# Dilated-window attention into a token/channel mixer: batch 2's q and k turned by DMA transposes, and batch 2's steps placed anew

## The chip, the cores and the metric

One core of one Trainium2 chip. The metric is the device time of one execution in microseconds (us), the median of the runs. Inputs and output are float32 in DRAM; inside, the kernel works in float16 with float32 sums in PSUM.

## What is computed

Batch 8, 8 heads, 576 positions, head size 64 (512 channels). The reference, cut to what matters:

```python
scores = matmul(q, k.T) / 8                       # per batch and head
rel = i - j                                       # heads 0-3: 0 <= rel < 32
                                                  # heads 4-7: 0 <= rel < 128 and rel % 4 == 0
attn = softmax(where(mask, scores, -1e9))
x = attn @ v                                      # [8, 576, 512], heads side by side
h = relu(x.T @ w_tok1) @ w_tok2                   # mixes positions, 576 -> 256 -> 576
u = x + h.T
out = u + relu(u @ w_ch1) @ w_ch2                 # mixes channels, 512 -> 1536 -> 512
```

## The kernel before, in words

The work goes batch by batch, and all engines but TensorE work ahead of or behind it. For one batch b:

- **Loads.** SP issues the loads of q, k (tiles `l_q`, `l_k`, two halves of four heads each, and `lt` for the last 64 positions) and of v (`l_vn`, four DMAs; `l_vt`, the last 64 positions; `l_vd`; `l_vx`), lines 187 to 245. The weights w_ch1 (`w3`, in thirds) and w_ch2 (`w4`, in thirds, `load_w4`, line 983) are issued by POOL, which casts to float16 on the way.
- **Casts.** `cast_steps` (line 275) gives 17 casts to float16, all on POOL: the tails of q and k, then q and k of the four head pairs in turn, then the eight of v.
- **Turns.** q and k are wanted with the head's channels on partitions. Batches 0 and 1 use `transposes` (line 304) on TensorE. Batch 2 uses `turn_steps` (line 406): `unpad` (line 381) makes four TensorE transposes for each of q and k of the four head pairs and copies them from PSUM by ACT or DVE; `turn_tails` (line 396) does the tails. Batches 3 to 7 use `dma_steps` (line 348): five DMA transposes on SP's queue (tails, then q and k of head pairs 0 and 1, then of 2 and 3), and `place_steps` (line 367): six copies by POOL that put the keys into order.
- **Scores.** For b of 2 and more, `scores_twin` (line 509) runs twice: g = 0 for head pairs 0 and 1 (plain window), g = 1 for pairs 2 and 3 (dilated). It takes six PSUM banks: two of `sc`, three of `fl`, one of `main`. ACT makes eight exps of it, then POOL multiplies by the masks (`mask`, line 566).
- **Values** (line 589): 8 heads, matmuls by TensorE, a reciprocal and a product by DVE. **Token mix**: `emit_h1` (line 618) and `emit_u` (line 629), where "summed" says that x is added by an identity matmul on TensorE and ACT copies, instead of an addition on DVE. For b of 2 and more u is turned by a DMA transpose (`uT_dma`), and `uT_place` has ACT copy half of it into order (line 697).
- **Channel mix.** `gen_first` (line 746): 12 blocks mb of `gp` matmuls (line 767), each into one `main` bank, with a relu on ACT or DVE (line 770); in odd batches three groups `gt` (line 758) for the tails of two batches. `gen_second` (line 776): `yp` chains of 12 matmuls over all of w4, an addition by DVE and the store by SP. The three `main` banks go round in turn.

**What sets the order.** Each engine takes its instructions in the order in which the program emits them. The channel mix is a generator that yields after each piece what the piece costs TensorE; `interleave` (line 819) adds these up as t and emits a step when t has reached the step's place:

```python
steps = sorted(steps, key=lambda st: st[0])
...
    if steps and (main is None or steps[0][0] <= t):
        _, cost, fn = steps.pop(0)
        fn()
        t += cost
```

So a step's place sets its position in the lists of all engines that it uses, the DMA queues of SP and POOL among them. The pass around the change is `firsts()` (line 1007): the first half of batch 1's channel mix, then the second halves of batches 0 and 1, with batch 2's casts, turns, scores, values and token mix, and batch 3's casts, turns and scores placed between (lines 1012 to 1024). The pass ahead of it (lines 1000 to 1005) runs `gen_first(0)` with batch 1's turns, scores, values and token mix between. From line 1030 on one loop does batches 2 to 7.

Of the kernel before, what the change touches and what calls it, by code (L numbers as in the profile page):

```python
# [69 lines left out]
def kernel(  # L70
# [11 lines left out]
    nc = tc.nc  # L82
    sb = ctx.enter_context(tc.tile_pool(name="sb", bufs=1))
    ps = ctx.enter_context(tc.tile_pool(name="ps", bufs=1, space=bass.MemoryType.PSUM))
    SRC = {"q": q, "k": k, "v": v}

    def fixed(name, shape, dtype=FP16):
# [168 lines left out]
    def cast_tails_qk(b, eng):  # L256
        c16[(b, "t")] = sb.tile([128, H, D], FP16, tag="c_t", bufs=1, name=f"c_t_{b}")
        copy(eng, c16[(b, "t")], l32[(b, "t")])

    def cast_tail_v(b, eng):  # L260
        copy(eng, vv[b % 2][0:64, 4, :, 0:64], l32[(b, "vt")])
# [10 lines left out]
    def cast_vx(b, eng):  # L272
        copy(eng, vt[b % 2][:, :, 0:64], l32[(b, "vx")])

    def cast_steps(b, eng=nc.gpsimd):
        steps = [lambda: cast_tails_qk(b, eng)]
        for hp in range(4):
            for nm in ("q", "k"):
                steps.append(lambda nm=nm, hp=hp: cast_qk(b, nm, hp, eng))
        for s in range(4):  # L280
            steps.append(lambda s=s: cast_vn(b, s, nc.gpsimd))
        steps.append(lambda: cast_tail_v(b, nc.gpsimd))
        for h in (0, 2):
            steps.append(lambda h=h: cast_vd(b, h, nc.gpsimd))
        steps.append(lambda: cast_vx(b, nc.gpsimd))
        return steps


# [220 lines left out]
    def scores_twin(b, g):  # L509
# [56 lines left out]
        def mask(hp):  # L566
            if g == 0:
                w = plain_blocks(hp)[:, :, :, 0:BLK]
                mult(nc.gpsimd, w, w, band)
            else:  # L570
                w = attd[hp - 2].rearrange("p h (r c) -> p h r c", c=128)
                mult(nc.gpsimd, w, w, band[:, :, :, 0:128])

        main(2 * g)
        if g:
# [5 lines left out]
        if not g:  # L581
            mask(0)
        t = tail_cols(slice(2 * g, 2 * g + 2), g)
        mult(nc.gpsimd, t, t, tails_seen[g])
        if not g:
            mask(1)
        yield 0.0
# [30 lines left out]
    def emit_h1(b, jb, half, t):  # L618
        x = xn[b]
        j = slice(jb, DTOK, 2)  # L620
        c = slice(256 * half, 256 * half + 256)
        w = w1p if half else w1n
        p = bank("fl", 3, f"h1p_{b}_{jb}_{half}")[:, 0:256]
        nc.tensor.matmul(out=p, lhsT=w1t[b % 2][:, j], rhs=x[:, 4, c], start=True, stop=False)  # L624
        for s in range(4):
            nc.tensor.matmul(out=p, lhsT=w[:, s, j], rhs=x[:, s, c], start=False, stop=(s == 3))  # L626
        relu(nc.vector if jb and (b == 1 or (b == 0 and half)) else nc.scalar, t[:, c], p)

    def emit_u(b, s, h1):
        p = bank("fl", 3, f"up_{b}_{s}")  # L630
        if s < 4:
            summed = b == 1 and s in (0, 2)
            for half in range(2):
                c = slice(256 * half, 256 * half + 256)
                if summed:
# [110 lines left out]
    def gen_first(b):  # L746
# [17 lines left out]
        for mb in range(NMB):  # L764
            p = bank("main", 3, f"gp_{b}_{mb}")
            for i, cb in enumerate(order):
                nc.tensor.matmul(out=p, lhsT=w3_block(cb, mb), rhs=uT[(b, cb)][0], start=(i == 0), stop=(i == 3))  # L767
                if i == 1:
                    yield 0.43
            relu(nc.vector if (mb % 2 == 1 if b == 0 else mb in (1, 5)) else nc.scalar, gta[:, mb, m0:m0 + 512], p)  # L770
            yield 0.43
            if odd and mb in (3, 6, 9):
                gp_tails(mb // 3 - 1)
                yield 0.9
# [168 lines left out]
    def u_half(s, half):  # L943
        p = bank("main" if half else "fl", 3, f"up_0_{s}_{half}")[:, 0:256]
        c = slice(256 * half, 256 * half + 256)
        t = u16(0, s)[:, 2 * half:2 * half + 2]
        summed = s in (0, 2)
        if summed:
            nc.tensor.matmul(out=p, lhsT=ident, rhs=xn[0][:, s, c], start=True, stop=False)
        for jb in range(2):  # L950
# [39 lines left out]
    for i in (0, 1, 2, 3, 4, 5, 7, 6, 8, 9, 10, 11, 12, 13, 14, 15, 16):  # L990
        casts1[i]()
        if i == 1:
            load_w3(2)
        if i in (14, 15, 16):
            load_w4(next(w4s))

    def at(t0, dt, fs):
        return [(t0 + dt * i, 0.0, f) for i, f in enumerate(fs)]

    steps = score_steps(1, 0, 0, (0.0, 0.6, 0.7), (  # L1000
        (2.9, 5.0), (4.2, 6.9), (5.4, 9.3), (8.0, 12.2)))
    va = value_steps(1, 11.3, 0.5)
    steps += va[:4] + [(p + 0.4, c, f) for p, c, f in va[4:]]
    steps += mix_steps(1, 16.0, 17.0, 18.0, 22.6, 0.6)
    interleave(gen_first(0), steps)

    def firsts():
# [1 line left out]
        yield from gen_second(0)  # L1009
        yield from gen_second(1)  # L1010

    steps = at(0, 0.0, [lambda: emit_loads_qk(2)]) + at(1.0, 0.0, [lambda: load_v(2)])
    casts = cast_steps(2)
    steps += at(0, 0.9, casts[:9]) + at(5.8, 0.1, casts[9:])
    steps += turn_steps(2, (5.0, 4.8, 4.2, 6.0, 8.0, 10.3, 9.2, 12.5, 7.9, 7.0),
                        (nc.scalar, nc.vector, nc.scalar, nc.vector, nc.scalar, nc.vector, nc.vector, nc.vector))
    steps += score_steps(2, 10.5, 4.6)
    va = value_steps(2, 19.5, 1.2)
    steps += va[:4] + [(p + 0, c, f) for p, c, f in va[4:]]
    steps += mix_steps(2, 25.5, 29.0, 29.0, 37.0)  # L1020
    steps += at(13.0, 0.0, [lambda: emit_loads_qk(3)]) + at(18.0, 0.0, [lambda: load_v(3)])
    steps += at(18.2, 0, cast_steps(3)) + at(23.0, 0.6, dma_steps(3)) + at(27.0, 0.5, place_steps(3))
    steps += score_steps(3, 35.5, 7.0) + at(33.4, 1.5, load_steps(4))
    interleave(firsts(), steps)

    def both(b):
# [44 lines left out]
```

## Time and profile before

| | |
|---|---|
| median of 3 runs | 286.7 us (286.6 to 286.73) |
| profiled execution | 286.81 us, span 285.0 us |
| PE busy | 273.8 us, 2760 matmuls |
| DVE busy | 132.3 us |
| ACT busy | 131.4 us |
| POOL busy | 166.8 us |
| DMA read, written in HBM | 37.05 MB, 9.44 MB |

The span runs from the first to the last instruction that the profiler shows; the 1.81 us between it and the execution's own time lie around it. PE is TensorE, DVE VectorE, POOL GpSimd, SP SyncE, which issues most DMAs. Times in the rows are us from the span's start unless marked ns. A matmul's duration in a row overlaps the next one's, so the distance between starts tells what it costs. In DMA rows the last number is the time from issue to landing.

### The profile page before, as it was taken

How to read it: one execution, taken by the hardware profiler on the slowest of the kernel's cores; microseconds unless marked ns; L12 is line 12 of the kernel's file. 1: busy time of each engine (PE TensorE's matmuls, PEld its weight loads, DVE VectorE, ACT ScalarE, POOL GpSimd, SP SyncE). 2: the span in 40 equal slices, each digit the busy share in tenths (PEclk: the TensorE clock that was granted, in tenths of full speed). 3: DMA queues.
4: the chain of work that ended last, by engine and by line, in shares of the span. 5: the costliest groups of instructions: out<-in, count | busy, mean ns of one | idle time of the engine just before them, and what ended most of it. 6: DMA issues, size and time to landing. Idle time of an engine off the chain costs nothing.

```text
span 285.0 us, 6873 instructions
## 1 busy us (share of the span) xinstructions
PE 273.8 (96%) x2760; PEld 207.0 (73%) x2760; DVE 132.3 (46%) x280; ACT 131.4 (46%) x263; POOL 166.8 (59%) x236
## 2 busy tenths in 40 slices
PE   5799899999999999999999999999999999999994
PEld 2696576676896976598776976797767966886594
DVE  6875687652365155514730263526531184322022
ACT  2964563458412374473446625482456435134500
POOL 7980853383998769769945998289945900000000
PEclk9999999999999999999999999999999999999999
DMA  7999999999658999999798989399994310521032
GB/s 217 262 227 253 269 230 241 273 223 307 165 105 191 147 332 274 190 168 352 201 191 191 319 241 188 60 235 314 207 148 83 110 39 0 111 93 37 2 86 99
DMA packets 105423, 52.60 MB, mean 185 GB/s; under 512 B 73872, under 2 KB 104208, under 8 KB 105392
## 3 DMA queue, kind: packets, MB, share of 16 engines
q1 hardware_dynamic: 101280, 47.07, 71.2%
q0 software_dynamic: 2512, 3.92, 7.6%
q10 hardware_dynamic: 1600, 1.18, 1.4%
q8 instruction: 21, 0.34, 0.5%
q14 instruction: 10, 0.08, 0.1%
HBM read 37.05 MB, written 9.44 MB: 163 GB/s over the span
## 4 chain that ended last, share of the span: by engine, by line
PE 79%; DMA 9%; POOL 4%; ACT 2%; DVE 2%; issue 1%; SPq 1%; ACTq 0%; POOLq 0%
PE gp L767 26%; PE yp L790 26%; PE h1p L626 4%; PE up L638 4%; PE gt L758 4%; PE yp L810 4%; DMA l_k<-in_k_dram 3%; DMA lt<-in_k_dram 3%; PE sc L519 2%; DMA utm<-u 2%; DMA w<-in_moe_w_tok_dram 2%; POOL attd L113 1%; PE av L605 1%; PE h1p L624 1%; PE av L600 1%
## 5 line engine op out<-in xcount | busy, mean ns | idle before, releaser
L790 PE MATMUL yp<-w,gt 128*128 128x256 f16 x756 | 86.5, 273 | 0.0
L790 PEld LDWEIGHTS <-gt 128*128 128x128 f16 x768 | 78.4, 106 | 6.2
L107 ACT ACTIVATE gt<-gp 128x512 f16<-128x512 f32 x76 | 45.4, 601 | 68.6 <-PE gp L767 68.3
L767 PE MATMUL gp<-utm,w 128*128 128x512 f16 x192 | 67.7, 379 | 0.0
L767 PE MATMUL gp<-utd,w 128*128 128x512 f16 x144 | 54.8, 380 | 0.0
L767 PEld LDWEIGHTS <-w 128*128 128x128 f16 x384 | 39.0, 114 | 20.4 <-issue 1.9
L800 DVE TENSOR_TENSOR o<-yp,u 128x512 f32<-128x512 f32 x31 | 21.4, 691 | 66.5 <-PE yp L790 64.6
L113 POOL TENSOR_TENSOR attp<-attp,const 128x1280 f16<-128x1280 f16 x12 | 31.4, 2615 | 22.4 <-ACT attp L545 18.0
L113 DVE TENSOR_TENSOR xn<-av,rec 128x320 f16<-128x320 f32 x64 | 31.5, 492 | 2.2
L113 POOL TENSOR_TENSOR attd<-attd,const 128x1024 f16<-128x1024 f16 x12 | 25.3, 2129 | 2.4 <-ACT attd L545 2.4
L644 DVE TENSOR_TENSOR u<-up,xn 128x512 f16<-128x512 f32 x26 | 17.5, 689 | 14.1 <-PE up L638 14.0
L103 POOL CAST c_k<-l_k 128x512 f16<-128x512 f32 x29 | 18.0, 623 | 8.8 <-PE tpu L675 7.6
L107 ACT ACTIVATE h<-h1p 128x256 f16<-128x256 f32 x29 | 11.1, 383 | 26.0 <-PE h1p L626 25.7
L103 POOL CAST c_q<-l_q 128x512 f16<-128x512 f32 x31 | 19.6, 635 | 2.6 <-DMA l_q<-in_q_dram 2.6
L545 ACT ACTIVATE attp<-sc 128x480 f16<-128x480 f32 (+1 forms) x36 | 16.1, 528 | 7.4 <-PE sc L519 7.4
L109 DVE TENSOR_SCALAR gt<-gp 128x512 f16<-128x512 f32 x20 | 13.7, 686 | 10.1 <-PE gp L767 10.1
L103 POOL CAST vv<-l_vn 128x256 f16<-128x256 f32 (+1 forms) x40 | 15.0, 403 | 4.0 <-DMA l_vn<-in_v_dram 3.5
L373 POOL COPY kt<-kr 128x512 f16<-128x512 f16 x10 | 10.8, 1079 | 10.4 <-DMA kr<-c_k 6.6
L697 ACT COPY utd<-utm 128x512 f16<-128x512 f16 x12 | 12.7, 1123 | 9.0 <-DMA utm<-u 9.0
L615 DVE RECIPROCAL rec<-av 128x5 f32<-128x5 f32 x64 | 12.2, 190 | 7.4 <-PE av L612 7.0
L545 ACT ACTIVATE attd<-sc 128x512 f16<-128x512 f32 x24 | 12.4, 604 | 6.1 <-PE sc L519 6.1
L758 PEld LDWEIGHTS <-w 128*128 128x128 f16 x192 | 11.9, 113 | 2.0 <-issue 0.4
(149 smaller groups left out, 441.2 us busy)
## 6 DMA issues: line engine op xcount, KB each, us to landing
out_dram<-o SPq DMA_DIRECT2D x72, 128.0 KB, 2.7
l_q<-in_q_dram SPq DMA_DIRECT2D x15, 512.0 KB, 6.9
l_k<-in_k_dram SPq DMA_DIRECT2D x14, 512.0 KB, 7.4
l_vn<-in_v_dram SPq DMA_DIRECT2D x32, 128.0 KB, 6.7
l_vd<-in_v_dram SPq DMA_DIRECT2D x16, 256.0 KB, 4.3
w<-in_moe_w_ch_dram POOLq DMA_DIRECT2D x6, 512.0 KB, 8.3
lt<-in_q_dram SPq DMA_DIRECT2D x8, 128.0 KB, 5.0
l_vt<-in_v_dram SPq DMA_DIRECT2D x8, 128.0 KB, 4.6
```

Source lines behind the costliest of these rows:

```text
L103: eng.tensor_copy(out=out, in_=in_)
L107: nc.scalar.activation(out=out, in_=in_, func=AF.Relu)
L109: eng.tensor_scalar_max(out=out, in0=in_, scalar1=0.0)
L113: eng.tensor_tensor(out=out, in0=x, in1=y, op=ALU.mult)
L545: nc.scalar.activation(out=out, in_=in_, func=AF.Exp, scale=0.125)
L615: nc.vector.reciprocal(out=rec[:, :, 0], in_=av[:, :, 64])
L644: nc.vector.tensor_tensor(out=u16(b, s), in0=blocks4(p), in1=blocks4(xn[b][:, s]), op=ALU.add)
L697: nc.scalar.copy(out=natural(uTd[:, cb - 2]), in_=uTm[i][:, cb].rearrange("p r m -> p m r"))
L758: nc.tensor.matmul(out=p[:, 128 * i:128 * i + 128], lhsT=w3_block(cb, 4 * g + i), rhs=uT[(b, cb)][1], start=(cb == order[0]), stop=(cb == ...
L767: nc.tensor.matmul(out=p, lhsT=w3_block(cb, mb), rhs=uT[(b, cb)][0], start=(i == 0), stop=(i == 3))
L790: nc.tensor.matmul(out=p[:, c], lhsT=gta[:, mb, a0:m0 + 512:4] if half else gta[:, mb, a0:a0 + 128], rhs=w4[mb][:, c], start=(mb == 0), st ...
L800: nc.vector.tensor_tensor(out=blocks4(o32), in0=blocks4(p), in1=u16(b, s), op=ALU.add)
```

## The change

q and k of batch 2 are turned by `dma_steps` and `place_steps`, as in later batches. In the order of emission of the new pass, batch 2's loads of q and k come first, then the nine casts of q and k, the second third of w4, the five turns, the six key copies, the last third of w4, then the loads of v and its casts, of which the tail's is on DVE. (Before, all three thirds of w4 were issued within the casts of batch 1's v, and batch 2's v was loaded right behind its q and k.) One of batch 2's plain masks goes from POOL to DVE. Relus of the channel mix are dealt anew between ACT and DVE: for batch 0, DVE has mb 1 instead of the six odd ones; for batch 1, the six odd ones instead of 1 and 5; later 1, 7, 9 instead of 1 and 5. The relus of the token mix are all ACT's. Identity matmuls stand in u of batch 0 for s = 0, 2, 3 (was 0, 2) and of batch 1 for s = 2 (was 0, 2). The places of the steps are new in both passes.

```diff
--- before.py
+++ after.py
@@ -82,6 +82,7 @@
     nc = tc.nc
     sb = ctx.enter_context(tc.tile_pool(name="sb", bufs=1))
     ps = ctx.enter_context(tc.tile_pool(name="ps", bufs=1, space=bass.MemoryType.PSUM))
+    DVE, ACT, POOL = nc.vector, nc.scalar, nc.gpsimd
     SRC = {"q": q, "k": k, "v": v}
 
     def fixed(name, shape, dtype=FP16):
@@ -272,17 +273,17 @@
     def cast_vx(b, eng):
         copy(eng, vt[b % 2][:, :, 0:64], l32[(b, "vx")])
 
-    def cast_steps(b, eng=nc.gpsimd):
-        steps = [lambda: cast_tails_qk(b, eng)]
+    def cast_steps(b, engs=(nc.gpsimd,) * 17):
+        steps = [lambda: cast_tails_qk(b, engs[0])]
         for hp in range(4):
             for nm in ("q", "k"):
-                steps.append(lambda nm=nm, hp=hp: cast_qk(b, nm, hp, eng))
+                steps.append(lambda nm=nm, hp=hp: cast_qk(b, nm, hp, engs[2 * hp + 1 + (nm == "k")]))
         for s in range(4):
-            steps.append(lambda s=s: cast_vn(b, s, nc.gpsimd))
-        steps.append(lambda: cast_tail_v(b, nc.gpsimd))
-        for h in (0, 2):
-            steps.append(lambda h=h: cast_vd(b, h, nc.gpsimd))
-        steps.append(lambda: cast_vx(b, nc.gpsimd))
+            steps.append(lambda s=s: cast_vn(b, s, engs[9 + s]))
+        steps.append(lambda: cast_tail_v(b, engs[13]))
+        for i in range(2):
+            steps.append(lambda i=i: cast_vd(b, 2 * i, engs[14 + i]))
+        steps.append(lambda: cast_vx(b, engs[16]))
         return steps
 
 
@@ -566,10 +567,10 @@
         def mask(hp):
             if g == 0:
                 w = plain_blocks(hp)[:, :, :, 0:BLK]
-                mult(nc.gpsimd, w, w, band)
+                mult((POOL, DVE)[hp] if b == 2 else POOL, w, w, band)
             else:
                 w = attd[hp - 2].rearrange("p h (r c) -> p h r c", c=128)
-                mult(nc.gpsimd, w, w, band[:, :, :, 0:128])
+                mult((POOL, POOL)[hp - 2] if b == 2 else POOL, w, w, band[:, :, :, 0:128])
 
         main(2 * g)
         if g:
@@ -581,7 +582,7 @@
         if not g:
             mask(0)
         t = tail_cols(slice(2 * g, 2 * g + 2), g)
-        mult(nc.gpsimd, t, t, tails_seen[g])
+        mult((POOL, POOL)[g] if b == 2 else POOL, t, t, tails_seen[g])
         if not g:
             mask(1)
         yield 0.0
@@ -624,12 +625,12 @@
         nc.tensor.matmul(out=p, lhsT=w1t[b % 2][:, j], rhs=x[:, 4, c], start=True, stop=False)
         for s in range(4):
             nc.tensor.matmul(out=p, lhsT=w[:, s, j], rhs=x[:, s, c], start=False, stop=(s == 3))
-        relu(nc.vector if jb and (b == 1 or (b == 0 and half)) else nc.scalar, t[:, c], p)
+        relu(nc.vector if jb and (b < 0) else nc.scalar, t[:, c], p)
 
     def emit_u(b, s, h1):
         p = bank("fl", 3, f"up_{b}_{s}")
         if s < 4:
-            summed = b == 1 and s in (0, 2)
+            summed = b == 1 and s in (2,)
             for half in range(2):
                 c = slice(256 * half, 256 * half + 256)
                 if summed:
@@ -767,7 +768,7 @@
                 nc.tensor.matmul(out=p, lhsT=w3_block(cb, mb), rhs=uT[(b, cb)][0], start=(i == 0), stop=(i == 3))
                 if i == 1:
                     yield 0.43
-            relu(nc.vector if (mb % 2 == 1 if b == 0 else mb in (1, 5)) else nc.scalar, gta[:, mb, m0:m0 + 512], p)
+            relu(nc.vector if mb in ((1,), (1, 3, 5, 7, 9, 11), (1, 7, 9))[min(b, 2)] else nc.scalar, gta[:, mb, m0:m0 + 512], p)
             yield 0.43
             if odd and mb in (3, 6, 9):
                 gp_tails(mb // 3 - 1)
@@ -944,7 +945,7 @@
         p = bank("main" if half else "fl", 3, f"up_0_{s}_{half}")[:, 0:256]
         c = slice(256 * half, 256 * half + 256)
         t = u16(0, s)[:, 2 * half:2 * half + 2]
-        summed = s in (0, 2)
+        summed = s in (0, 2, 3)
         if summed:
             nc.tensor.matmul(out=p, lhsT=ident, rhs=xn[0][:, s, c], start=True, stop=False)
         for jb in range(2):
@@ -991,17 +992,17 @@
         casts1[i]()
         if i == 1:
             load_w3(2)
-        if i in (14, 15, 16):
+        if i in (14,):
             load_w4(next(w4s))
 
     def at(t0, dt, fs):
         return [(t0 + dt * i, 0.0, f) for i, f in enumerate(fs)]
 
-    steps = score_steps(1, 0, 0, (0.0, 0.6, 0.7), (
-        (2.9, 5.0), (4.2, 6.9), (5.4, 9.3), (8.0, 12.2)))
+    steps = score_steps(1, 0, 0, (0.0, 0.6, 1.5), (
+        (2.9, 5.8), (5.0, 7.7), (6.6, 9.3), (8.0, 11.4)))
     va = value_steps(1, 11.3, 0.5)
     steps += va[:4] + [(p + 0.4, c, f) for p, c, f in va[4:]]
-    steps += mix_steps(1, 16.0, 17.0, 18.0, 22.6, 0.6)
+    steps += mix_steps(1, 16.0, 17.0, 18.0, 30.6, 0.0)
     interleave(gen_first(0), steps)
 
     def firsts():
@@ -1009,18 +1010,18 @@
         yield from gen_second(0)
         yield from gen_second(1)
 
-    steps = at(0, 0.0, [lambda: emit_loads_qk(2)]) + at(1.0, 0.0, [lambda: load_v(2)])
-    casts = cast_steps(2)
-    steps += at(0, 0.9, casts[:9]) + at(5.8, 0.1, casts[9:])
-    steps += turn_steps(2, (5.0, 4.8, 4.2, 6.0, 8.0, 10.3, 9.2, 12.5, 7.9, 7.0),
-                        (nc.scalar, nc.vector, nc.scalar, nc.vector, nc.scalar, nc.vector, nc.vector, nc.vector))
-    steps += score_steps(2, 10.5, 4.6)
-    va = value_steps(2, 19.5, 1.2)
-    steps += va[:4] + [(p + 0, c, f) for p, c, f in va[4:]]
-    steps += mix_steps(2, 25.5, 29.0, 29.0, 37.0)
-    steps += at(13.0, 0.0, [lambda: emit_loads_qk(3)]) + at(18.0, 0.0, [lambda: load_v(3)])
-    steps += at(18.2, 0, cast_steps(3)) + at(23.0, 0.6, dma_steps(3)) + at(27.0, 0.5, place_steps(3))
-    steps += score_steps(3, 35.5, 7.0) + at(33.4, 1.5, load_steps(4))
+    steps = at(0.0, 0.0, [lambda: emit_loads_qk(2)]) + at(6.0, 7.5, [lambda: load_v(2)])
+    casts = cast_steps(2, (POOL, POOL, POOL, POOL, POOL, POOL, POOL, POOL, POOL, POOL, POOL, POOL, POOL, DVE, POOL, POOL, POOL))
+    steps += at(0.0, 0.0, casts[:9]) + at(6.5, 0.0, casts[9:])
+    steps += at(0.0, 5.5, [lambda: load_w4(next(w4s))]) + at(5.4, 0.0, [lambda: load_w4(next(w4s))])
+    steps += at(2.0, 0.5, dma_steps(2)) + at(5.1, 0.0, place_steps(2))
+    steps += score_steps(2, 10.0, 3.1)
+    va = value_steps(2, 18.7, 1.2)
+    steps += va[:4] + [(p + 0.0, c, f) for p, c, f in va[4:]]
+    steps += mix_steps(2, 26.6, 29.1, 30.1, 43.0)
+    steps += at(9.5, 6.5, [lambda: emit_loads_qk(3)]) + at(15.5, 0.0, [lambda: load_v(3)])
+    steps += at(17.2, 0, cast_steps(3)) + at(21.0, 0.0, dma_steps(3)) + at(27.0, 0.5, place_steps(3))
+    steps += score_steps(3, 35.0, 4.5) + at(38.4, 0.5, load_steps(4))
     interleave(firsts(), steps)
 
     def both(b):
```

## Rows read from the trace of the kernel before

**Rows 1.** The page's first part: busy time, share of the span, instructions.
```profile
PE 273.8 (96%) x2760; PEld 207.0 (73%) x2760; DVE 132.3 (46%) x280; ACT 131.4 (46%) x263; POOL 166.8 (59%) x236
```
**Rows 2.** Stretches: length, busy PE, PEld, DVE, ACT, POOL (instructions), clock, DMA share, GB/s.
```profile
26.00:54.00 28.00, 26.44 (x292) 18.29 (x290) 20.22 (x45) 13.92 (x29) 13.19 (x25) 1.00 1.12 253
54.00:72.00 18.00, 17.40 (x184) 11.48 (x182) 6.92 (x15) 12.42 (x26) 11.25 (x19) 1.00 1.10 268
...
103.00:280.00 177.00, 176.87 (x1686) 133.13 (x1685) 71.65 (x148) 80.03 (x156) 98.76 (x123) 1.00 0.71 164
```
**Rows 3.** Timeline of TensorE, batch 1's first half: start, us, line, shapes, count.
```profile
54.62 3.71 PE L767 MATMUL gp<-uT,w 128*128 128x512 f16 x16
...
59.07 0.39 PE L385 MATMUL tp_q<-const,c_q 128*128 128x128 f16 x4
59.29 0.59 PE L767 MATMUL gp<-uT,w 128*128 128x512 f16 x2
```
**Rows 4.** Timeline of TensorE, batch 2's scores to batch 3's [idle before <-what ended it].
```profile
66.08 0.23 PE L519 MATMUL sc<-qt,kt 64*128 64x128 f16 x2 [0.20 <-DVE kt L103]
...
68.67 1.05 PE L758 MATMUL gt<-uT,w 128*128 128x128 f16 x16 [0.18 <-ACT attt L545]
...
72.08 3.44 PE L790 MATMUL yp<-w,gt 128*128 128x256 f16 x30
...
91.28 0.65 PE L519 MATMUL sc<-qt,kt 64*128 64x160 f16 x14
```
**Rows 5.** Timeline of TensorE, batch 1's turns in the pass before.
```profile
31.61 0.40 PE L310 MATMUL tp_k<-const,c_k 128*128 128x128 f16 x4 [0.20 <-POOL c_k L103]
32.16 0.40 PE L310 MATMUL tp_q<-const,c_q 128*128 128x128 f16 x4 [0.16 <-POOL c_q L103]
...
34.98 0.38 PE L310 MATMUL tp_k<-const,c_k 128*128 128x128 f16 x4 [0.26 <-DVE kt L103]
```
**Rows 6.** Timeline of ACT: batch 2's first exps, and u's copies ahead of batch 3's.
```profile
65.77 2.23 ACT L545 ACTIVATE attp<-sc 128x480 f16<-128x480 f32 x5
...
99.59 2.08 ACT L697 COPY utd<-utm 128x512 f16<-128x512 f16 x2 [4.98 <-DMA utm<-u]
```
**Rows 7.** DMA issues one by one, 39 to 57 us: queue, size, us to landing.
```profile
l_k<-in_k_dram SPq DMA_DIRECT2D x1, 512.0 KB, 13.6
...
w<-in_moe_w_ch_dram POOLq DMA_DIRECT2D x1, 512.0 KB, 8.2
...
w<-in_moe_w_ch_dram POOLq DMA_DIRECT2D x1, 512.0 KB, 11.8
...
l_vt<-in_v_dram SPq DMA_DIRECT2D x1, 128.0 KB, 4.7
```
**Rows 8.** Timeline of POOL: w4's first third, batch 2's first k, batch 3's first key copy.
```profile
41.33 0.54 POOL L984 DMA_DIRECT2D w<-in_moe_w_ch_dram  x1 [0.19 <-issue]
...
53.62 0.61 POOL L103 CAST c_k<-l_k 128x512 f16<-128x512 f32 x1 [7.58 <-PE tpu L675]
...
88.57 1.06 POOL L373 COPY kt<-kr 128x512 f16<-128x512 f16 x1
```
**Rows 9.** SP: turns (issue ns min/median/max) and landing; four vn; batch 4's turns' stretch.
```profile
L351 SPq DMA_TRANSPOSE qt<-c_q x10: 1253/1455/2196, 81.9 to 206.7; - x10
...
DMA to landing us min/median/max: 3.1/3.9/5.7
...
4.52 3.18 SPq L206 DMA_DIRECT2D l_vn<-in_v_dram  x4
...
112.00:119.00 7.00, 7.00 (x46) 4.26 (x45) 3.26 (x6) 3.30 (x7) 5.47 (x12) 1.00 1.12 219
```
**Rows 10.** The page's fifth part: relus on DVE, busy, mean ns, idle before.
```profile
L109 DVE TENSOR_SCALAR gt<-gp 128x512 f16<-128x512 f32 x20 | 13.7, 686 | 10.1 <-PE gp L767 10.1
```
**Rows 11.** Timeline of POOL and TensorE: batch 3's dilated masks and their first value.
```profile
102.73 4.22 POOL L113 TENSOR_TENSOR attd<-attd,const 128x1024 f16<-128x1024 f16 x2 [2.39 <-ACT attd L545]
...
108.12 0.20 PE L609 MATMUL av<-vt,attt 128*128 128x65 f16 x1
```

## Prediction

> **What bounds the kernel now.** I read the page first, then stretches, then each engine's timeline between 26 and 125 us. TensorE is busy for 96% of the span [rows 1], and from 103 to 280 us for 176.87 of 177.00 us [rows 2]: once batch 2's pass has begun, TensorE has no gap to give. So the end moves by two things alone: work taken from TensorE's list, and waits of TensorE that vanish or appear. Before 103 us there are waits: 1.56 us of idle in 26:54 and 0.60 us in 54:72 [rows 2]. Most edits lie here, and the DMA engines are full here (share 1.12 and 1.10 [rows 2]). So I ask what the edits do to TensorE's list and its waits, and whether the DMA queues can deliver in time. The granted clock is 1.00 in every stretch [rows 2], the 2.4 GHz level, and nothing in the change leaves TensorE idle for long; I leave the clock out. One caution: an idle figure of TensorE counts from the modelled end of the matmul before. Four transposes that began at 31.61 should have let the next start at 31.83; it started at 32.16 with 0.16 of idle shown [rows 5]. So 0.33 us was lost: the idle figure plus 0.17. I add that 0.17 to each wait.
>
> **1. The turns leave TensorE: -2.0 us.** Batch 2 is turned by 32 transposes for q and k and 4 for the tails. A group of four starts at 59.07 and the next matmul at 59.29 [rows 3]: 0.22 us a group, nine groups, 2.0 us. The 0.39 us of the row overlaps its neighbours. They stand amid gp matmuls that run without a pause, so the whole is on the path. The Trainium skill, page "TensorE: Matmul & The Clock Gate", section on PE-mode transpose, measures about 275 ns for one transpose in a kernel; 36 would be 9.9 us and the time 277.1. The rows give 0.055 us each, so the trace disagrees, and I take the rows.
>
> **2. Waits that go with the turns: -0.7 us.** Batch 2's first scores wait at 66.08 for a key copy by DVE (0.20 + 0.17), and the gt group at 68.67 for a bank that ACT's exps hold (0.18 + 0.17) [rows 4]. Whether they come back is part 4.
>
> **3. Batch 1's steps: -0.75 us.** TensorE meets q of head pair 1 at 32.16 (0.33 lost) and k of pair 2 at 34.98 (0.26 + 0.17) [rows 5]. The new places put gp matmuls ahead of both. The wait for the very first k (31.61) stays, because POOL's cast sets it. The relus moved from DVE to ACT cost nothing: ACT is busy 13.92 of 28.00 us in 26:54, DVE 20.22 [rows 2], and five relus more make ACT 17. The identity matmuls are two fewer in batch 1 and two more in batch 0: zero. Batch 0's two lie ahead of TensorE's wait for POOL's first cast of batch 1; the two fewer lie where DVE now adds one more u and holds the bank. The relus that stand on DVE for mb 1, 7, 9 in later batches are off the path.
>
> **4. A new wait at batch 2's scores: +1.8 us.** The tail cast of v goes from POOL to DVE, which takes its instructions in order. What such a wait does, ACT shows at 99.59: it sat 4.98 us for a DMA, with the next exps behind it [rows 6]. When does the tail land? SP issues batch 2's loads, then the five turns, then v. Without two of the three w4 loads beside them, q and k come sooner: k's first half took 13.6 us with w4 in flight [rows 7], which is why POOL's cast ran only at 53.62 [rows 8] (the profile names PE there, but the load landed at that moment). The first w4 (issued at 41.33 [rows 8], 8.2 us [rows 7]) still shares until 49.5, so I put that half at 50.0 and the last at 53.7 (2.0 us per 512 KB at the 253 GB/s of [rows 2]). Three casts later, at 55.4, SP may issue the last turn. A turn costs SP 1.25 to 1.46 us; two follow the cast of q at 54.9, so v begins near 57.5. Its four vn take 3.2 us [rows 9], the tail is issued at 60.6, and 4.7 us later [rows 7] it is here: about 65.2. Then come its cast and, behind it on DVE, the relu of gp 7, at 0.69 each by DVE's nearest row of 512 columns [rows 10]: 66.6. That relu frees the bank which batch 2's small scores want, as the third user after it in the turn of three. The pass begins at 54.62 - 0.75 = 53.9 [rows 3], and by the placing rule TensorE is there 10.9 us later, at 64.8. So it waits 1.8 us. I bound the landing by 63.5 (if k's last half were here at 52) and 66.5 (if the tail took 6 us). There is a floor of 0.8: if v is early, gp 11 waits instead for the bank of the small scores. ACT's eight exps, begun at 65.77, held it until the gt group could start at 68.67 [rows 4, 6], some 2.85 us, and only 1.8 us of matmuls will stand between in place of 2.3. The two overlap, so part 4 is 0.8 to 3.1, not their sum.
>
> **5. The turns by DMA: 0.** Scores want the keys at 64.4. The first halves of q and k are issued by 54.3 and land within 3.9 us of their issue [rows 9], near 57; POOL's copies took under 2.8 us in batch 3 (begun at 88.57 [rows 8], scores at 91.28 [rows 4]), so they end near 60. Cover: 4 us. The last w4 is issued behind those copies, at about 60.5, and lands 8.2 to 11.8 us later [rows 7], at 68.7 to 72.3; its first use is at 72.08 - 1.65 + 0.87 = 71.3 [rows 4]: 0 taken, up to 1.0 kept for the range. The turns also take the DMA engines' time: batch 4's five, with hardly anything beside them, filled the engines from 112 to 119 (share 1.12 [rows 9]). So I let batch 3's loads come 6 us later, its v near 82.5. POOL, with one mask less ahead of them, is at these casts earlier than before and waits for v; I put its last v cast at 86; the key copies (under 2.8 us) end near 89, ahead of 91.5.
>
> **6. POOL and what follows: 0.** One mask goes from POOL to DVE; its price there is not in the trace. By the nearest row, 0.69 for 512 columns [rows 10], 1280 would be 1.7 us; below, half of that; above, double. All are covered, because its values come some 7 us later. In the new order batch 3's scores stand behind three more yp pieces (0.65 us each by the placing rule), so they start 0.3 us after the old 91.28 [rows 4] and POOL has 2 us to spare. Its dilated masks no longer wait for ACT's copies. POOL was free at 102.73 - 2.39 = 100.34, worked until 108.1, 5.3 us in all, and would now end at 105.6. TensorE got them at 108.12 [rows 11], after 0.30 us of waiting, and would now ask at 108.12 - 0.30 - 1.65 = 106.17. Zero, with half a microsecond to spare.
>
> **Sum.** -2.0 - 0.7 - 0.75 + 1.8 = -1.65 us. The profiled execution took 286.81 us (span 285.0, 1.81 around it), which gives 285.16; the median of the runs is 0.11 below the profiled one, so **285.0 us**.
>
> **Rivals.**
> - *Slower: v's tail holds DVE.* Same place as part 4, but v lands so late that the wait eats everything. The gains are 3.45; with 0.57 us (0.2%) for a verdict the wait must pass 4.0 us, the landing 67.4. For it: a transfer of batch 2 took 13.6 us before [rows 7]; against it: the tail took 4.7. At a landing of 69 TensorE waits 5.6 us: 288.8. The Trainium skill, "DMA: Bandwidth & Descriptors", section "Queues, rings and completion order", says that a DMA engine takes turns between its queues packet by packet. By that rule the second w4, issued near 55.5 from POOL, would share with v; k's 13.6 us agrees. Chance 0.12.
> - *w4 late.* TensorE waits for the last third in the first yp chain, 0.5 to 1.5 us: 285.5 to 286.5. For it: 11.8 us once [rows 7]; against it: that was the last of three in a row. Chance 0.12.
> - *The gain isn't carried.* POOL has 0.5 us of reserve at batch 3's masks and 2 us at its keys. If batch 3's loads come 3.5 us later still, TensorE stands at batch 3's scores for 1.2 us: 286.2. Chance 0.12.
> - *It doesn't do what it says:* the transposes only filled waits, so taking them out shows as waits. Then only part 3 is left against part 4: 286.7 - 0.75 + 1.8 = 287.7. Against it: the groups follow one another without a gap [rows 3]. Chance 0.04.
> - *The transposes cost their rows' full time:* nine groups of 0.39 are 3.5 us instead of 2.0, 283.5. Against it: [rows 3] show them overlapping. Chance 0.01.
>
> **How the numbers follow.** The forecast has 0.59, the other cases 0.41. A measurement of this kernel can tell about 0.2%, 0.57 us, from no change, so faster is below 286.13. The forecast's own range is 283.5 (part 4 at 0.8, with half a microsecond of waits elsewhere gone) to 286.3 (part 4 at 3.1). With the w4 rival and the third, 283.5 to 286.8 leaves out 2 in 10. Faster: 0.56 of the forecast, 0.09 of w4, 0.05 of the third, 0.01 of the last: 0.71. Same: 0.03, 0.03, 0.06 and 0.01 of the first: 0.13. Slower: the rest, 0.16.
>
> **What would show it.** Right: no transposes in batch 2's rows; a DVE cast of v's tail that waits for its DMA, and one TensorE wait of 1 to 3 us at batch 2's small scores; the first yp near 70.4 (72.08 before [rows 4]); the same lead of 1.6 us to the end. Wrong: a wait at the first yp (w4), at batch 2's first scores (turns late), at batch 3's scores or dilated values (POOL), or a lead that shrinks after 103 us.

## The result, and the profile after

The changed kernel takes 290.65 us in the median of 6 runs (289.64 to 291.49), the kernel before 286.59 in runs beside it; ratio 1.0147, 95% interval 1.0124 to 1.017. It is slower by 4 us, outside the range that was given. The profiled execution is the fastest of the six, 289.64 us, with a span of 287.9 us. Here and below a time is the median of all runs of a kernel, and a ratio leaves out a run that is over 1.5% above its kernel's fastest (one each in experiments 2 and 10).

The page's first part; it answers to [rows 1]:

```profile
PE 273.7 (95%) x2724; PEld 207.0 (72%) x2724; DVE 131.0 (45%) x273; ACT 128.3 (45%) x259; POOL 167.3 (58%) x240
```

36 matmuls fewer: the turns are gone from TensorE. Its busy time is nearly unchanged, since part of the work now ran at a lower clock (below). The stretches (columns as in [rows 2]), with two short ones between:

```profile
26.00:54.00 28.00, 27.02 (x307) 19.40 (x306) 18.25 (x42) 17.96 (x38) 15.93 (x30) 1.00 1.19 257
54.00:72.00 18.00, 14.43 (x115) 8.60 (x113) 5.82 (x9) 7.34 (x17) 7.24 (x16) 0.94 1.11 185
...
70.00:73.00 3.00, 3.00 (x15) 1.07 (x14) 0.83 (x1) 1.34 (x3) 0.90 (x2) 0.50 1.19 243
73.00:74.00 1.00, 1.00 (x26) 0.80 (x21) 0.00 (x0) 0.56 (x2) 0.96 (x2) 0.90 1.10 331
...
103.00:280.00 177.00, 176.12 (x1679) 132.22 (x1677) 74.69 (x154) 76.28 (x148) 99.97 (x124) 1.00 0.69 165
```

The loss lies in 54:72: TensorE idles 3.6 of 18 us (0.60 before), and the clock falls. The last two columns say where to look: the DMA engines are as busy as before (1.11, before 1.10) but move 185 GB/s, not 268. That is 18 us x 83 GB/s = 1.5 MB less, 5.6 us of the old rate. Not all of it is the turns' doing, since the second third of w4 now lies in this stretch too. Experiment 7, with w4 there and no turns, moves 254, and experiment 3, with the turns and w4 early, 201. The turns' own bytes are in the 185, and they bring in nothing from DRAM. A share of 1.11 doesn't mean that no engine stood idle either: in the first half microsecond of the stretch nothing moved, while SP was issuing a turn. SP's timeline shows what stood behind them:

```profile
48.29 2.56 SPq L352 DMA_TRANSPOSE qt<-c_q  x1
...
54.80 1.27 SPq L352 DMA_TRANSPOSE kr<-c_k  x1
56.13 6.23 SPq L207 DMA_DIRECT2D l_vn<-in_v_dram  x4
62.41 0.62 SPq L207 DMA_DIRECT2D l_vt<-in_v_dram  x1
```

The last turn was issued at 54.80, earlier than the prediction had it (v from 57.5 on; it began at 56.13). But the four vn cost SP 6.23 us, so the tail of v went out at 62.41. The 3.18 of [rows 9] are from the start of the kernel (4.52 us). The same trace has two more rows for four vn, of batches 2 and 3, with busy DMA engines (share 1.06 in 44:54, 1.08 in 63:72) and no turn beside them:

```profile
43.07 12.86 SPq L206 DMA_DIRECT2D l_vn<-in_v_dram  x4
...
64.65 5.39 SPq L206 DMA_DIRECT2D l_vn<-in_v_dram  x4
```

So 6.23 is no odd price for this stretch, and not by itself a sign of the turns. DVE, which casts that tail:

```profile
60.30 0.69 DVE L110 TENSOR_SCALAR gt<-gp 128x512 f16<-128x512 f32 x1 [1.03 <-PE gp L768]
67.55 0.55 DVE L104 CAST vv<-l_vt 64x512 f16<-64x512 f32 x1 [6.57 <-DMA l_vt<-in_v_dram]
68.03 1.26 DVE L110 TENSOR_SCALAR gt<-gp 128x512 f16<-128x512 f32 x2
```

It sat 6.57 us for the load, with a relu behind the cast for which the TensorE bank waited. TensorE, with the same stretch of work as [rows 4]:

```profile
64.53 0.64 PE L520 MATMUL sc<-qt,kt 64*128 64x160 f16 x13
68.75 0.21 PE L520 MATMUL sc<-qt,kt 64*128 64x128 f16 x1 [3.57 <-DVE gt L110]
...
70.04 2.77 PE L768 MATMUL gp<-uT,w 128*128 128x512 f16 x6
72.74 0.82 PE L520 MATMUL sc<-qt,kr 64*128 64x128 f16 x16
...
74.07 2.13 PE L791 MATMUL yp<-w,gt 128*128 128x256 f16 x18
...
123.57 0.44 PE L520 MATMUL sc<-qt,kt 64*128 64x160 f16 x8 [0.88 <-POOL kt L374]
```

TensorE is at the small scores about when forecast (65.2, that is 68.75 less the wait; 64.8) and stands 3.57 us. From 70 to 73 us the granted clock is 0.50, the 1.2 GHz level, with 0.89 in the microsecond before and 0.90 in the one behind: six gp matmuls take 2.77 us, where sixteen took 3.71 [rows 3]. The wait had ended at 68.75, about a microsecond before the fall; nothing else had stopped TensorE since 54. At half clock 3 us hold 1.5 us of work, and with 0.1 lost on either side this costs 1.7 us. One more wait, 0.88 us, follows at batch 4's keys. After it the two traces run alike.

**The account**, in distances within each trace, since the first turn of batch 1 (30.09 before, 30.55 after) starts at a moment that the first loads set:

| stretch of TensorE | before | after | difference |
|---|---|---|---|
| first turn of batch 1 to first gp of batch 1 | 24.53 | 23.38 | -1.15 |
| to the first yp | 17.46 | 20.14 | +2.68 |
| to batch 2's first gp | 31.18 | 30.79 | -0.39 |
| to batch 3's first gp | 29.07 | 29.91 | +0.84 |
| to the end | 148.96 | 148.97 | 0.0 |

The sum is +1.98, with 0.46 from the later start +2.44; the execution is 2.83 longer, and the 0.4 between them lie behind TensorE's last matmul. The forecast had -0.9 in the second line (-2.0 - 0.7 + 1.8). The 3.6 us that it misses there are the wait, 3.57 + 0.17 in place of 1.8, and the clock, 1.7.

### The profile page after: what moved, and what is told of

Same layout as the page of the kernel before. It is cut to its first block, busy times and chain, and to the rows that moved or that the text cites. A ratio compares the mean times of both kernels' runs of the same rounds, so it can differ in the third digit from the quotient of the medians.

```text
span 287.9 us, 6801 instructions
## 1 busy us (share of the span) xinstructions
PE 273.7 (95%) x2724; PEld 207.0 (72%) x2724; DVE 131.0 (45%) x273; ACT 128.3 (45%) x259; POOL 167.3 (58%) x240
## 4 chain that ended last, share of the span: by engine, by line
PE 72%; DMA 14%; SPq 4%; POOL 4%; DVE 2%; issue 1%; ACT 1%; POOLq 0%; ACTq 0%
PE yp L791 26%; PE gp L768 21%; DMA l_vd<-in_v_dram 4%; DMA l_k<-in_k_dram 4%; PE yp L811 4%; PE h1p L627 4%; PE gt L759 3%; PE up L639 3%; PE sc L520 3%; SPq L207 3%; DMA const<-consts 2%; DMA l_vt<-in_v_dram 2%; DMA l_q<-in_q_dram 2%; DMA kr<-c_k 1%; SPq L807 1%
## 5 line engine op out<-in xcount | busy, mean ns | idle before, releaser
L108 ACT ACTIVATE gt<-gp 128x512 f16<-128x512 f32 x71 | 42.3, 597 | 75.3 <-PE gp L768 74.8
L114 POOL TENSOR_TENSOR attp<-attp,const 128x1280 f16<-128x1280 f16 x11 | 28.8, 2616 | 21.0 <-ACT attp L546 20.9
L110 DVE TENSOR_SCALAR gt<-gp 128x512 f16<-128x512 f32 x25 | 17.1, 686 | 30.9 <-PE gp L768 30.9
L108 ACT ACTIVATE h<-h1p 128x256 f16<-128x256 f32 x32 | 12.3, 383 | 24.3 <-PE h1p L627 23.6
L645 DVE TENSOR_TENSOR u<-up,xn 128x512 f16<-128x512 f32 x27 | 18.1, 686 | 1.3 <-PE up L639 0.8
L374 POOL COPY kt<-kr 128x512 f16<-128x512 f16 x12 | 12.9, 1075 | 9.5 <-DMA kr<-c_k 8.6
```

Of the source, the lines that this page charges most:

```text
L108: nc.scalar.activation(out=out, in_=in_, func=AF.Relu)
L110: eng.tensor_scalar_max(out=out, in0=in_, scalar1=0.0)
L114: eng.tensor_tensor(out=out, in0=x, in1=y, op=ALU.mult)
L374: nc.gpsimd.tensor_copy(out=natural(kt[hp][:, 0:512]), in_=kra[:, hp].rearrange("p r m -> p m r"))
L645: nc.vector.tensor_tensor(out=u16(b, s), in0=blocks4(p), in1=blocks4(xn[b][:, s]), op=ALU.add)
```

## The experiments

The theory at the start: v's tail lands late, because SP and the DMA engines are taken by the turns, and whoever waits for v hands the delay to TensorE. Rivals: DVE as the place of the cast is at fault; the order of w4 is; the turns only need to stand elsewhere; batch 4's loads are; or the turns are innocent.

**1. The tail's cast back on POOL.**

```diff
-    casts = cast_steps(2, (POOL, ..., DVE, POOL, POOL, POOL))
+    casts = cast_steps(2)
```

> Edit: the cast of batch 2's v tail goes back from DVE to POOL; all else as in the changed kernel (290.65 us, TensorE idle 3.57 us at batch 2's small scores, clock 0.50 at 70 to 73 us). Theory A, DVE's place in line alone: with DVE free the small scores wait at most 0.8 us, the clock stays at 1.00 and 3 us of waiting and 1.6 us of half clock come back: 285.5 to 286.5 us. Theory B, v is late for whoever waits for it: POOL's v casts end near 73 as now, its masks of batch 2 come behind them (73 to 81.6), and TensorE waits at the values instead, 1.2 us at the first and some 1.6 us at the first dilated one: 288 to 289.5 us.

291.15 us, ratio 1.0164 [1.0114, 1.0213]: no gain, and above both theories' ranges. The profile is of the quickest of the four runs (289.17); the others lie from 290.94 on. TensorE's timeline has no wait for DVE, but these, and two of 1.0 us for POOL's copies of batch 4's keys:

```profile
67.23 0.59 PE L768 MATMUL gp<-uT,w 128*128 128x512 f16 x2 [0.74 <-ACT attt L546]
...
70.45 3.87 PE L791 MATMUL yp<-w,gt 128*128 128x256 f16 x34 [0.53 <-DMA w<-in_moe_w_ch_dram]
...
75.52 0.20 PE L601 MATMUL av<-vv,attp 128*128 128x65 f16 x1 [1.20 <-POOL attp L114]
...
81.42 0.20 PE L610 MATMUL av<-vt,attt 128*128 128x65 f16 x1 [0.94 <-POOL attt L114]
```

The first is the floor of 0.8 that the prediction gave. The waits for POOL's masks are the same delay of v, now passed on by POOL, whose masks stand behind its casts of v. So the wait at DVE was the form of the loss, not its cause.

**2. v ahead of the turns.**

```diff
-    steps = ... + at(6.0, 7.5, [lambda: load_v(2)])
+    steps = ... + at(0.0, 7.5, [lambda: load_v(2)])
```

> Edit: batch 2's v is loaded right behind its q and k, ahead of the five turns, the tail cast still on DVE. By both theories v's tail lands near 60 and DVE does not wait. The turns then stand behind v in SP's list: if SP is held by full queues until about 58, the last turns are issued near 62 and POOL's key copies end near 66 to 68, so TensorE waits 2 to 4 us at the first scores (idle named after POOL kt): 288 to 291 us. If the turns had room after all, no wait: 284.5 to 286 us.

294.35 us (four runs from 291.65 to 297.73), 1.0258 [1.0168, 1.0348], slower than the 288 to 291 expected. Now the turns are late: in the trace TensorE waits 2.95 and 0.95 us at batch 2's scores for POOL's key copies, and 2.04 for w4, and the granted clock of 54:72 is 0.88. Either of these two orders makes something late.

**3. All of w4 early, as before.**

```diff
-        if i in (14,):
+        if i in (14, 15, 16):
```

> Edit: all three thirds of w4 are issued within batch 1's casts, as before the change; all else as changed. Theory C, the second third of w4 sharing the engines with turns and v is what made v late: the last turn lands in 4 instead of 8.2 us, the tail lands near 65 to 66, the wait shrinks by 1.5 to 2 us: 288 to 289 us. Theory D, the line at SP is what made v late: q and k land near 57 again, the casts end near 59, the turns are issued until 60.5, the tail lands near 69 and DVE holds TensorE for 1 to 3 us more: 291.5 to 294 us.

290.75 us, 1.0148 [1.0117, 1.0179]: no difference that can be measured, with 4.9 us of wait for DVE in its trace. Neither range (288 to 289, 291.5 to 294) was met. The stretch and SP's timeline:

```profile
54.00:72.00 18.00, 13.12 (x108) 8.51 (x107) 5.21 (x8) 6.79 (x15) 11.60 (x22) 0.87 1.12 201
```

```profile
54.71 1.35 SPq L352 DMA_TRANSPOSE qt<-c_q  x1
...
61.42 2.91 SPq L207 DMA_DIRECT2D l_vn<-in_v_dram  x4
64.37 0.63 SPq L207 DMA_DIRECT2D l_vt<-in_v_dram  x1
```

Both theories were right in part, and the parts cancel. With w4 out of the way the last turn landed in 4.5 us (8.2 in the changed kernel), the four vn cost 2.91 (6.23), and the tail landed in 3.9 (5.1): near the prediction's prices (3.9, 3.2 and 4.7), though the turns were directly ahead. But w4 now lay beside q and k: the first turn of q went out at 54.71, not 48.29, and the tail at 64.37, not 62.41. So w4 beside the last turns and v is part of what makes v late, and to move it to this place doesn't help.

**4. The tail on POOL, batch 2's large masks on DVE.**

```diff
-                mult((POOL, DVE)[hp] if b == 2 else POOL, w, w, band)
+                mult(DVE if b == 2 else POOL, w, w, band)
...
-                mult((POOL, POOL)[hp - 2] if b == 2 else POOL, w, w, band[:, :, :, 0:128])
+                mult(DVE if b == 2 else POOL, w, w, band[:, :, :, 0:128])
...
+    casts = cast_steps(2)
```

> Edit: as e1, and both plain and both dilated masks of batch 2 on DVE, so that no mask but the tails' stands behind v on POOL. Theory B: the waits at scores and at the plain values are both gone; left is the wait for POOL's tail masks at the values: 285 to 287 us, 2 us or more below e1. Theory A: the masks were not the bound, so the same as e1 within 0.5 us.

291.6 us, 1.0188 [1.0132, 1.0245]; the theory missed its 285 to 287. The profile is of the slowest of the four runs (293.58). POOL's waits at the values are gone, and what was behind them shows: TensorE stands 2.20 us for w4 at its first yp (72.50), then 2.8 us for batch 4's keys.

**5. Batch 4's loads at their old places.**

```diff
-    steps += score_steps(3, 35.0, 4.5) + at(38.4, 0.5, load_steps(4))
+    steps += score_steps(3, 35.0, 4.5) + at(33.4, 1.5, load_steps(4))
```

> Edit: batch 4's loads go back to their old places (33.4, one step every 1.5) from (38.4, every 0.5); all else as changed. Theory E, a second loss behind 103 us: in the changed kernel SP issued batch 4's loads 98.74 to 113.9 us, its turns behind them, and TensorE lost 0.88 us of idle at batch 4's scores (POOL's key copy). With the old places that wait is gone and the time falls by about 1 us, to 289.0 to 290.0 us; the wait at batch 2's scores stays 3 to 4 us. Rival: the turns of batch 4 are late because the whole of POOL and SP is late since batch 2, then the wait stays and the time is 290 to 291 us.

290.85 us, 1.015 [1.0126, 1.0173], with the same two waits (3.9 and 0.9 us). What makes batch 4's keys late by 0.9 us is not the place of its loads.

**6. The first pass's edits alone, on the kernel before** (the relus, the identity matmuls, the places of batch 1's steps).

```diff
-        relu(nc.vector if jb and (b == 1 or (b == 0 and half)) else nc.scalar, t[:, c], p)
+        relu(nc.vector if jb and (b < 0) else nc.scalar, t[:, c], p)
...
-            summed = b == 1 and s in (0, 2)
+            summed = b == 1 and s in (2,)
...
-        (2.9, 5.0), (4.2, 6.9), (5.4, 9.3), (8.0, 12.2)))
+        (2.9, 5.8), (5.0, 7.7), (6.6, 9.3), (8.0, 11.4)))
```

> Edit: the kernel before, with the change's edits of the pass ahead of batch 2 alone: batch 1's steps placed anew, relus of batch 0 and of the token mixes to ACT, the identity matmuls re-dealt. The changed kernel began the next pass 0.69 us earlier (53.93 for 54.62). If that lead is carried to the end: 285.6 to 286.1 us. Rival: POOL's list for batches 2 and 3 is fixed and takes the lead away: 286.3 to 286.7 us.

286.01 us in 12 runs, 0.9979 [0.9966, 0.9991], against 286.47: part 3 of the prediction is worth 0.46 us at the end.

**7 and 8. No turn of batch 2 at all**, in the new order and in the old; the scores read tiles that POOL fills with zeros. The places in 7, then in 8:

```diff
-    steps += at(2.0, 0.5, dma_steps(2)) + at(5.1, 0.0, place_steps(2))
+    steps += at(5.1, 0.0, place_steps(2))
...
-    steps += turn_steps(2, ...)
+    steps += at(7.0, 0.0, [lambda: ends(nc.vector)])
```

> Edit: the changed kernel with batch 2's five DMA transposes left out (its scores read a blank tile that POOL sets to zero while it is idle near 22 us), everything else in place. Theory B, the transposes fill the DMA engines and SP's line when these are full, and whatever is behind them comes late: v lands 4 to 6 us earlier, DVE's tail cast and POOL's masks do not wait, no wait but the 0.8 us floor is left at batch 2's scores: 284.0 to 286.0 us. Rival, the order of w4, v and the casts is at fault and not the transposes: v's tail still lands after 66 and the time is 288 us or more.

> Edit: the kernel before with batch 2's turns left out altogether, the 36 transposes of TensorE and the copies out of PSUM (the same blank tiles). This is the most that any way of turning batch 2 off TensorE can give: 2.0 us of transposes and 0.7 us of waits, 283.5 to 284.3 us. Rival: POOL and DMA set the pace behind TensorE, and less than 1 us comes back: 285.6 us or more.

The new order without turns: 285.8 us, 0.999 [0.9963, 1.0016]. With them the ratio was 1.0147, so the five DMA turns, as placed, cost 1.6%, 4.5 us (4.85 by the medians). The runs lie in two groups, five of 284.27 to 285.26 and five of 286.34 to 287.89, so this is a mean; the profile is of the second (287.44). Its stretch and SP's timeline:

```profile
54.00:72.00 18.00, 16.85 (x166) 10.74 (x164) 8.49 (x11) 10.34 (x22) 11.88 (x20) 1.00 1.10 254
```

```profile
44.99 8.16 SPq L207 DMA_DIRECT2D l_vn<-in_v_dram  x4
53.24 1.04 SPq L207 DMA_DIRECT2D l_vt<-in_v_dram  x1
```

The tail was issued at 53.24 and landed 4.8 us later; in the changed kernel at 62.41 and 5.1. So what the turns take from v is almost all time in SP's line: there SP comes to v at 56.13, and here at 44.99, since it needn't wait for the casts of q and k and issue five turns. The four vn cost even more here, 8.16 us.

The old order without turns: 285.94 us, 0.9985 [0.9966, 1.0003]. So in the old order, to take the turns off TensorE for nothing brings some 0.5 us, not clear of noise, where the prediction counted 2.7. (In the new order the quicker five runs of experiment 7 are 1.2 to 2.2 us below the kernel before; what sets them apart, no trace shows.) TensorE's waits after 54 us in the trace of experiment 8:

```profile
PE yp L790 <- ACT attt L545: 0.9, 1, 0.9
PE sc L519 <- POOL kt L373: 0.7, 1, 0.7
PE av L609 <- POOL attt L113: 0.5, 1, 0.5
```

There ACT's exps, POOL's masks and batch 4's keys stand right behind TensorE. With 0.17 for each wait they take 2.6 of the 2.7 us.

**9. v issued by POOL, not behind the turns on SP.**

```diff
-    steps = ... + at(6.0, 7.5, [lambda: load_v(2)])
+    steps = ... + at(5.0, 7.5, [lambda: load_v(2, POOL)])
...
```

> The changed kernel, but batch 2's eight loads of v are issued by POOL ahead of its key copies, not by SP behind the five turns. Theory L (v is late because it stands in SP's line behind the turns): v's tail is issued near 57 instead of 62.4 and lands near 62 to 63, DVE's cast is in time, the 3.6 us wait at batch 2's small scores shrinks to the 0.7 that ACT's exps set, the clock stays at 1.00, and the time is 286 to 287. Theory E (the turns take the DMA engines' own time, whoever issues beside them): v's tail comes earlier, but the last turn, which landed at 63.0, comes later by about as much, TensorE waits for batch 2's keys instead, and the time stays within 289.5 to 292.

299.03 us, 1.0432 [1.0402, 1.0462]. Theory L fell. E was right that the last turn comes later, but the tail came later too, TensorE still waited for DVE (7.16 us), and the time is far beyond E's range. POOL issued the tail at 57.1. From issue to landing, from the view of the tile of v's tail and that of the turned keys:

```profile
DMA to landing us min/median/max: 14.3/14.3/14.3
...
DMA to landing us min/median/max: 3.3/11.3/19.4
```

And its stretch:

```profile
54.00:72.00 18.00, 10.47 (x82) 6.20 (x81) 3.27 (x6) 5.65 (x10) 8.72 (x13) 0.89 1.10 128
```

The tail took 14.3 us (5.1 in the changed kernel) and the last turn 19.4 (8.2). Out of SP's line both are later still: the engines move 128 GB/s at the same share. So to take v out of SP's line does not by itself bring it early; turns and loads beside one another slow each other. But one thing more moved with v: SP went on to batch 3's loads at 55.78 us, not 65.65, so these lay beside v and the last turn as well. The Trainium skill, page "DMA: Bandwidth & Descriptors", section "Queues, rings and completion order", has an engine take turns between its queues packet by packet; that both kinds of transfer are stretched agrees with it. How much of it is POOL's queue itself, and how much batch 3's loads, no run here separates.

**10. Three turns by DMA, q and k of pairs 2 and 3 by TensorE.**

```diff
-    steps += at(2.0, 0.5, dma_steps(2)) + at(5.1, 0.0, place_steps(2))
+    steps += at(2.0, 0.5, dma_steps(2)[:3]) + at(5.1, 0.0, place_steps(2)[:4])
+    steps += [(p, 0.24, lambda nm=nm, hp=hp, e=e: unpad(2, nm, hp, e)) for p, nm, hp, e in (
+        (8.0, "q", 2, ACT), (9.0, "k", 2, DVE), (9.2, "q", 3, DVE), (11.5, "k", 3, DVE))]
```

> The changed kernel, but only the tails and head pairs 0 and 1 of batch 2 are turned by DMA (three turns); q and k of pairs 2 and 3 are turned by TensorE as before, in four groups of 0.22 us (0.9 us on TensorE). If the cost grows with the turns (five cost 4.85 us): v's tail is issued some 2.5 us earlier, lands near 65, the wait at batch 2's small scores is 1 us or less, the clock stays at 1.00, and the time is 286.5 to 288. Rival (what delays v is the order of the steps or SP's wait for the casts, of which the first three turns suffice): the tail still lands at 67 or later and the time is 290 to 291.5.

The median of 10 runs is 289.06 us (1.0067 [1.003, 1.0105]), but four runs lie between 286.22 and 286.82 and six between 288.85 and 292.66. The profile is of one of the quick ones (286.58 us); its stretch, and then the cast of the tail in DVE's timeline:

```profile
54.00:72.00 18.00, 16.62 (x162) 10.57 (x160) 7.56 (x15) 10.51 (x23) 9.57 (x16) 1.00 1.05 222
```

```profile
63.17 0.42 DVE L104 CAST vv<-l_vt 64x512 f16<-64x512 f32 x1 [2.46 <-DMA l_vt<-in_v_dram]
```

There the tail was issued at 55.02, 7.4 us earlier than with five turns, took 8.1 us (5.1), and landed at 63.1, 4.4 us earlier; no wait of TensorE for that cast, no fall of the clock, and 222 GB/s lies between 254 without turns and 185 with five. So here too the tail gains in SP's line and not on its way. In this trace the theory holds, its time included. What the other six runs waited for, no trace shows; in five of them the mean granted clock was 0.986 to 0.993 (0.997 to 1.000 in the quick four), so it fell there as in the changed kernel. The median is above the 286.5 to 288 that the theory gave.

**11 and 12. The kernel of experiment 6, with the tail's cast on DVE and, in 11 alone, one mask as well.**

```diff
-        steps.append(lambda: cast_tail_v(b, nc.gpsimd))
+        steps.append(lambda: cast_tail_v(b, nc.vector if b == 2 else nc.gpsimd))
...
-                mult(nc.gpsimd, w, w, band)
+                mult((nc.gpsimd, nc.vector)[hp] if b == 2 else nc.gpsimd, w, w, band)
```

> The kernel before with the first pass's edits (286.0) and, in addition, the two placings on DVE: batch 2's tail cast of v and its second plain mask. v stands ahead here, no DMA turns. Theory (DVE's cast is harmless when v is early, and a mask off POOL is off the path): the tail lands near 62, no wait of TensorE for DVE, 285.5 to 286.3. Rival (the cast on DVE costs by itself, because DVE then stands for any load): a TensorE wait of over 1 us behind a DVE relu, 287 or more.

287.3 us, 1.003 [1.0012, 1.0047]: the theory missed. The rival has the time but not the cause: DVE's cast of the tail didn't wait. DVE, then POOL, in 11:

```profile
68.90 3.28 DVE L113 TENSOR_TENSOR attp<-attp,const 128x1280 f16<-128x1280 f16 x1 [2.53 <-ACT attp L545]
72.10 0.41 DVE L103 COPY kr<-tp_k 128x512 f16<-128x512 f16 x1
...
68.88 2.61 POOL L113 TENSOR_TENSOR attp<-attp,const 128x1280 f16<-128x1280 f16 x1 [2.63 <-PE gp L767]
```

In the changed kernel the same mask took DVE 0.83 us at 70.08, where POOL's masks began at 73.16. Here POOL's starts 0.02 us ahead of DVE's, and DVE's takes 3.28; the copy of keys behind it is late, and TensorE waits 1.3 us. The Trainium skill, page "SBUF — State Buffer", section "SBUF: two separate sides", says that DVE, in an instruction with two SBUF inputs, and GpSimd contend for one pair of ports by an exclusive lock: who starts first has it for the whole instruction, and the other is blocked. The row agrees: POOL's mask ends at 71.49, DVE's 0.69 us later, at 72.18.

> The kernel before with the first pass's edits (286.0), and batch 2's tail cast of v on DVE, but both plain masks on POOL as before. In the run with the mask on DVE as well, that mask took 3.28 us beside POOL's mask of 2.61, the copy of keys behind it came late and TensorE waited 1.3 us. Theory (the mask beside POOL's mask is what cost there): no such wait, 285.7 to 286.3. Rival (the cast on DVE ahead of the relus costs): the wait for DVE's copy stays, 287 or more.

285.51 us in 12 runs, 0.9968 [0.9951, 0.9985], with no such wait. The cast on DVE is harmless where v is early, and this is the lowest median of the study: 0.9 us below the kernel before and 5 below the changed one. Its interval overlaps that of experiment 6, so that the cast itself gains anything is not shown.

## Why the prediction was wrong

- **Part 4 is the step that failed, and the first rival is what happened.** Its place, its chain (tail, cast, relu, bank) and TensorE's arrival (65.2; 64.8) were right. Its size was not: the landing was put at 65.2, at most 66.5, and was 67.5. The term that was mis-sized is the issue of v by SP: v began 1.4 us earlier than forecast (56.13; 57.5), but the four vn at 3.2 us were 6.23, and the tail at 4.7 was 5.1. The 3.2 came from the start of the kernel, while rows of the same trace near this stretch have 12.86 and 5.39. Experiment 3 shows what lay beside v: with w4 issued early the same four vn, behind the same turns, cost 2.91. So the sharing with the second third of w4, which the rival named, is borne out, and part 4's own sum had no price for it. The turns' 7 us of DMA time were in the working, but in part 5, charged to batch 3's loads and not to v, which stands directly behind them; how much of the 6.23 is theirs stays open.
- **"I leave the clock out"** was the second mistake: 1.7 us. The sentence rested on there being no long wait, the very thing that part 4 left uncertain. The rival's price lacked it too: the sum with the measured wait of 3.74 in place of 1.8 gives 287.1, hardly above the kernel before; with 1.7 of clock and 0.88 + 0.17 at batch 4's keys it is 289.85, and 289.64 was measured.
- **Parts 1 and 2** (-2.7): the price of a turn, 0.055 us, is not contradicted, and in the changed kernel the wait and the clock account for all that the second line of the table misses. But the sum was not to be had without the wait either, in the old order: experiment 8 keeps 0.5 of it. Two rivals had the idea: "the gain isn't carried", with POOL at batch 3, and "it doesn't do what it says", in which work taken out shows as waits (chance 0.04). In experiment 8 the waits are for ACT and POOL, at batch 2's first yp and values already. That TensorE has no gap [rows 2] shows what bounds the kernel, and not how close the next is.
- **Part 3** (-0.75) held in the trace: 1.15 us from the first turn of batch 1 on, 0.69 after the later start. In experiment 6, 0.46 of it reached the end.
- **Part 5** (0): the keys of the first two pairs were ready at 57.3, earlier than the 60 that was forecast. The last turn took 8.2 us and not 3.9; POOL stood 5.81 us for it, and so issued the last third of w4 at 63.77, not 60.5. That did no harm, since TensorE came late itself: w4 caused no wait in this trace; when TensorE came earlier (experiments 1 and 4) it waited 0.53 and 2.20 us.
- **Part 6** (0): batch 3's masks caused no wait. One of 0.88 came at batch 4's keys, which the prediction did not look at. It stands in experiments 7 and 8 too (0.9 and 0.7), so the DMA turns are not its cause; what is, stays open.

The median is 1.0 us above the profiled execution. The mean granted clock was 0.994 in that one, 1.7 us of its span by this figure, and 0.988 to 0.991 in the other five, 2.6 to 3.5 us: by this estimate a longer fall of the clock is the difference. What made it longer, no trace shows.

## What to carry to other kernels

Work taken off a bound engine is worth only what the next engine leaves; leave the work out once, as in experiment 8, before paying for its removal. A DMA that moves data on the chip, and waits in the issuing engine's line for what makes that data, is to be charged to the loads behind and beside it: look at the moment of issue (62.41; 53.24 without turns), and at GB/s beside the share. Price a load by rows from its own stretch: four vn cost 3.18 us at the start of the kernel before, 12.86 and 5.39 near the stretch that counted. And an engine that works in order must not hold a cast of a load that may be late ahead of what frees a bank.

## What was not expected of the hardware

- At the same share of the engines (1.10 and 1.11) 18 us moved 254 GB/s without the DMA turns and 185 with them. One turn took 3.4 us or 8.2 from issue to landing, and 19.4 with v from POOL's queue and batch 3's loads beside it.
- A mask of 128x1280 float16 took DVE 0.83 us alone and 3.28 beside POOL's (2.61 for POOL).
- About a microsecond after a wait of 3.57 us had ended, the clock fell to 0.50 and stood there for 3 us.
- Ten runs of one kernel can lie in two groups some 2 us apart or more (experiments 7 and 10), so one profile shows one of them.
